# Hash-bucket attention and a channel mix on one core: the first two pairs of heads turned in float16 instead of float32, with a new written-out order

## The chip, the cores and the metric

The kernel runs on one core of one Trainium2 chip. The metric is the time of one execution on the device in microseconds (us), as the median of several runs. The engines are called TensorE (PE in the profile), VectorE (DVE), ScalarE (ACT), GpSimd (POOL) and SyncE (SP, which issues most of the DMAs).

## What is computed

The inputs `q`, `k`, `v` are 4 batches x 8 heads x 768 positions x 64 dimensions, in float32. Each row of `q` and `k` gets six bits, the signs of its products with the columns of `proj`; a row of `q` sees only those rows of `k` whose six bits are the same. The result goes through a channel mix with a squared ReLU and a gate.

```python
q_bits = np.einsum('bhsd,dk->bhsk', q, proj) > 0      # and k_bits in the same way
mask = q_bucket[:, :, :, None] == k_bucket[:, :, None, :]
scores = np.where(mask, q @ k.T / 8, -1e9)
x = softmax(scores) @ v                                # heads side by side: 768 x 512 per batch
xk, xr = mixes of x with x shifted by one position
out = sigmoid(xr @ w_r) * (relu(xk @ w_k) ** 2 @ w_v)
```

## The kernel before

**Pairs.** The work goes by 16 pairs of heads (`n` = 0 to 15, four pairs to a batch). A pair has a `q` side and a `k` side with two heads each (`j` = 0, 1). For each pair an operand tile `a` is made that holds, per head, dimensions down the partitions and 768 positions along the row, in float16. Partitions 0 to 63 hold the rounded value ("hi", for `q` and `k` alike four times the input). Of partitions 64 to 127, six hold the bits as large numbers of either sign, so that one product gives score and mask at once: where all six bits agree, a large constant is added, and `exp` with a bias takes it away again; where one differs, `exp` gives nothing.

**Making `a`, pairs 2 to 15.** `add_prep` (L390): VectorE writes "hi" (L398) and what the rounding left, "lo" (L401), into a tile `nh` with positions down the partitions; a DMA transpose (L405) turns `nh` into `a`. `add_bits` (L414): TensorE multiplies `a` (hi and lo) with the negated `proj`, in tiles of 32 columns side by side (L427), VectorE cuts the signs out of PSUM (L431, tile `bx`), and GpSimd copies six rows per head and side over rows of "lo" in `a` (L443), four copies a pair.

**Making `a`, pairs 0 and 1.** `add_prep_turn` (L446) does not use the DMA transpose: TensorE turns the float32 input (L478), ScalarE copies it out of PSUM (L483), TensorE multiplies it with `pw`, a float32 `proj` for two heads side by side (L489), VectorE cuts the signs (L497) straight into the places of the bits in `nh`, beside "hi" (L467), and TensorE turns `nh` in float16 (L512). VectorE or ScalarE copies that to `a` (L517, L519). So there are no row copies for these two pairs, and no "lo".

**Scores and attention.** `add_scores` (L530): nine steps a pair of 1024 columns of PSUM each (L544), and for each an `exp` on ScalarE (L548) that gives the step's PSUM banks free. `add_pv` (L556): the products with `v` and a column of ones (L571), division (L582 to L589), and the turn back (on TensorE for pairs 0 to 3 and 15, L599). The sums of `v` behind L566 and L374 are made by GpSimd (L350 to L362). `add_mix` (L623): the mixes `xk` and `xr` of a pair, on VectorE.

**Channel mix.** `add_moe` (L648), once a batch has its four pairs: `w_k` (L659), ReLU (L663), square (L666), `w_r` (L679), tanh (L682), `w_v` (L692), last product (L699), output DMA (L702).

**Order.** Every operation is recorded by `add` (L98) with its engine. `ORDER` (L17) is a list, written out, of all operations; each engine runs its own operations in that order and waits for what it depends on. `BANKS` (L72) gives each group of results its place in the eight banks of PSUM, so a product also waits until the place's former tenant has been read. In `ORDER` of the kernel before, the first product of `w_k` of batch 0 comes when 50 of the 144 score steps have been issued, and the score steps go on between the products after that. At the start and in a few places later TensorE multiplies zeros into an unused bank (L246, 14 times one product, and L251, eight times two).

Of the kernel before, what the change touches and what calls it, by code (L numbers as in the profile page):

```python
# [8 lines left out]
FP32 = mybir.dt.float32  # L9
FP16 = mybir.dt.float16  # L10
BF16 = mybir.dt.bfloat16
U16 = mybir.dt.uint16
# [57 lines left out]
]  # L70

BANKS = [  # L72
# [706 lines left out]
```

## Time and profile before

| what | value |
|---|---|
| median of three runs | 242.76 us (242.56 to 243.35) |
| the profiled execution | 242.0 us |
| its span, first to last instruction | 240.2 us |
| TensorE busy | 234.1 us |
| ScalarE busy | 181.9 us |
| VectorE busy | 179.8 us |
| GpSimd busy | 99.7 us |
| granted TensorE clock | 1.0 in every slice |

Around the span of the profiled execution lie 1.8 us, and it took 0.8 us less than the median. Busy time of TensorE is read with care: its matmuls overlap, and their ends are modelled, so what tells of TensorE is the distance from one matmul's start to the next. Rows of the chain of waits give that distance, since they are merged along the chain; rows of the groups give the mean of one instruction from start to end.

### The profile page before, as it was taken

The page shows a single profiled execution, that of the slowest core. Times are in us where ns is not written, and L with a number is a line of the kernel's source. Part 1 is how long each engine was busy: PE and PEld are TensorE (multiplying, and loading weights), DVE is VectorE, ACT ScalarE, POOL GpSimd, SP SyncE. Part 2 cuts the span into 40 slices and gives each one's busy share as a digit, 9 for nine tenths or more (in the row PEclk, how much of TensorE's full clock was granted, in tenths as well). Part 3 has the DMA queues.
Part 4 walks back from the last instruction along what each step waited for, and adds up shares of the span by engine and source line. Part 5 has one row for each costly group of instructions (what it writes and reads, how often), then busy time and mean ns, then how long its engine had stood idle before and what let it go on. Part 6 is the DMA issues. An engine that isn't in the chain of part 4 may idle for free.

```text
span 240.2 us, 6251 instructions
## 1 busy us (share of the span) xinstructions
PE 234.1 (97%) x2515; PEld 147.8 (62%) x2532; DVE 179.8 (75%) x388; ACT 181.9 (76%) x242; POOL 99.7 (41%) x148
## 2 busy tenths in 40 slices
PE   8999999999999999999999999999999999999994
PEld 6985776776766565656456656665566564455442
DVE  3488789999998898989868896887167867348232
ACT  2699999999999999889779999677884640256320
POOL 4064979989934899438087302550000000000000
PEclk9999999999999999999999999999999999999999
DMA  6989999999999999988999989401500401210333
GB/s 225 304 222 274 232 242 260 279 197 362 279 253 284 273 213 294 249 302 206 276 163 241 249 177 234 136 0 26 173 0 3 120 3 44 87 46 1 131 135 131
DMA packets 72605, 44.00 MB, mean 183 GB/s; under 512 B 54912, under 2 KB 67584, under 8 KB 72576
## 3 DMA queue, kind: packets, MB, share of 16 engines
q1 hardware_dynamic: 72208, 43.20, 70.9%
q8 instruction: 20, 0.33, 0.6%
q10 hardware_dynamic: 368, 0.39, 0.5%
q14 instruction: 9, 0.07, 0.1%
HBM read 24.12 MB, written 6.29 MB: 127 GB/s over the span
## 4 chain that ended last, share of the span: by engine, by line
PE 92%; ACT 5%; issue 1%; DVE 0%
PE ps_all L544 25%; PE ps_all L692 17%; PE ps_all L659 16%; PE ps_all L571 14%; PE ps_all L679 8%; ACT pt L548 4%; PE ps_all L427 4%; PE ps_all L489 2%; PE ps_all L512 1%; PE ps_all L478 1%; ACT kr L663 1%; PE ps_all L251 1%; PE ps_all L246 1%; PE ps_all L599 1%; PE ps_all L566 1%
## 5 line engine op out<-in xcount | busy, mean ns | idle before, releaser
L548 ACT ACTIVATE pt<-ps_all 128x1024 bf16<-128x1024 f32 x144 | 138.4, 1041 | 10.9 <-PE ps_all L544 10.3
L544 PE MATMUL ps_all<-a 128*128 128x256 f16 (+1 forms) x384 | 79.2, 325 | 0.5 <-ACT pt L548 0.3
L443 POOL COPY a<-bx 6x384 f32<-6x384 f32 x56 | 38.9, 695 | 34.4 <-DVE bx L431 19.6
L544 PEld LDWEIGHTS <-a 128*128 128x128 f16 x384 | 34.0, 98 | 23.5 <-issue 4.6
L659 PE MATMUL ps_all<-xk,wk 128*128 128x384 bf16 x256 | 48.3, 326 | 0.1
L571 PEld LDWEIGHTS <-pt 128*128 128x128 bf16 x1152 | 42.5, 97 | 8.0 <-issue 0.5
L692 PE MATMUL ps_all<-wv,k 128*128 128x512 bf16 (+2 forms) x199 | 45.6, 362 | 0.5
L571 PE MATMUL ps_all<-va,pt 128*128 128x65 bf16 x1152 | 44.8, 193 | 0.0
L663 ACT ACTIVATE kr<-ps_all 128x384 bf16<-128x384 f32 x64 | 29.4, 491 | 16.0 <-PE ps_all L659 14.4
L659 PEld LDWEIGHTS <-wk 128*128 128x128 bf16 x256 | 24.2, 98 | 17.0 <-issue 0.6
L692 PEld LDWEIGHTS <-k 128*128 128x128 bf16 x208 | 19.3, 98 | 18.9 <-issue 0.3
L699 DVE SCALAR_TENSOR_TENSOR os<-rs,ps_all 128x512 f32<-128x512 f32 (+2 forms) x26 | 16.5, 643 | 19.0 <-PE ps_all L692 13.7
L682 ACT ACTIVATE rs<-ps_all 128x512 f32<-128x512 f32 x24 | 14.3, 602 | 20.5 <-PE ps_all L679 14.1
L666 DVE TENSOR_TENSOR k<-kr 128x384 bf16<-128x384 bf16 x64 | 23.2, 389 | 8.3 <-ACT kr L663 8.3
L401 DVE SCALAR_TENSOR_TENSOR nh<-nat,nh 128x1536 f16<-128x1536 f32 (+1 forms) x16 | 27.0, 1694 | 0.2
L679 PE MATMUL ps_all<-wr,xr 128*128 128x512 bf16 x88 | 23.2, 379 | 0.4
L356 POOL TENSOR_TENSOR vt<-vn 128x384 f32<-128x384 f32 x12 | 17.8, 1485 | 12.5 <-DMA vn<-in_v_dram 11.7
L589 DVE TENSOR_TENSOR ob<-ps_all,rc 128x384 bf16<-128x384 f32 x32 | 17.5, 553 | 1.4 <-DMA xt<-ob 0.8
L431 DVE TENSOR_SCALAR bx<-ps_all 128x768 uint16<-128x768 uint16 x14 | 13.4, 956 | 5.3 <-PE ps_all L427 4.7
L398 DVE TENSOR_SCALAR nh<-nat 128x1536 f16<-128x1536 f32 (+1 forms) x16 | 15.8, 985 | 0.3 <-PE ps_all L512 0.2
L679 PEld LDWEIGHTS <-xr 128*128 128x128 bf16 x96 | 9.0, 98 | 9.0
L380 DVE SCALAR_TENSOR_TENSOR va<-ps_all,vn 128x384 bf16<-128x384 f32 x24 | 12.7, 548 | 0.5 <-PE ps_all L375 0.2
(77 smaller groups left out, 188.9 us busy)
## 6 DMA issues: line engine op xcount, KB each, us to landing
vn<-in_v_dram SPq DMA_DIRECT2D x16, 384.0 KB, 5.1
out_dram<-os SPq DMA_DIRECT2D x23, 256.0 KB, 2.3
nat<-in_k_dram SPq DMA_DIRECT2D x15, 384.0 KB, 4.7
nat<-in_q_dram SPq DMA_DIRECT2D x15, 384.0 KB, 5.2
wst<-in_moe_w_k_dram SPq DMA_DIRECT2D x2, 512.0 KB, 7.0
wst<-in_moe_w_r_dram SPq DMA_DIRECT2D x2, 512.0 KB, 5.8
wst<-in_moe_w_v_dram SPq DMA_DIRECT2D x2, 512.0 KB, 4.4
k<-in_moe_w_k_dram SPq DMA_DIRECT2D x1, 512.0 KB, 4.4
```

Of the source, the lines that this page charges most:

```text
L356: e.tensor_tensor(out=vt[:, :, :, 0:E], in0=src[:, :, 0:3, 0:E], in1=src[:, :, 3:6, 0:E], op=ALU.add)
L401: nc.vector.scalar_tensor_tensor(out=nh[:, :, D:P], in0=nat.rearrange("p j (c d) -> p (j c) d", d=D), scalar=QS, in1=nh[:, :, 0:D], op0=AL ...
L443: nc.gpsimd.tensor_copy(side_a[side][n % NAQ][D : D + NB, j, :].bitcast(FP32), bx_t[sx][32 * i : 32 * i + NB, :].bitcast(FP32))
L544: nc.tensor.matmul(ps[:, lo - s * STEP : hi - s * STEP], side_a["k"][sa][:, j, jc * P : (jc + 1) * P], side_a["q"][sa][:, j, q0 : q0 + hi ...
L548: nc.scalar.activation(out=pt_t[sp][:, s * STEP : (s + 1) * STEP], in_=ps_t[plan.slot[nm]], func=AF.Exp, bias=EBIAS, scale=ESC)
L571: nc.tensor.matmul(oo[:, ic * 65 : ic * 65 + 65], pt_t[sp][:, o : o + P], va_t[sa][:, j, jc, 0 : D + 1], start=(not uc and ic == 0 and jc ...
L589: nc.vector.tensor_tensor(out=ob_t[so][:, :, j * D : (j + 1) * D], in0=oo[:, :, 0:D], in1=rc_t[sr][:, 1, :].unsqueeze(2).to_broadcast([P, ...
L659: nc.tensor.matmul(ps[:, 0:HALF], wk_sb[:, d, fc * P : (fc + 1) * P], xk_t[mx[d]][:, h * HALF : (h + 1) * HALF], start=(d == 0), stop=(d = ...
L663: nc.scalar.activation(out=kr_t[sk], in_=sm(nm)[:, 0:HALF], func=AF.Relu, scale=0.5 ** 0.5)
L666: nc.vector.tensor_tensor(out=k2_t[s2][:, h * HALF : (h + 1) * HALF], in0=kr_t[sk], in1=kr_t[sk], op=ALU.mult)
L679: nc.tensor.matmul(sm(nr), xr_t[mx[d]][:, c * P : (c + 1) * P], wr_sb[:, d, :], start=(d == 0), stop=(d == NDC - 1))
L692: nc.tensor.matmul(sm(nv)[:, x0:x1], k2_t[(b * NFC + fc) % NK2][:, c * P : (c + 1) * P], wv_sb[:, fc, x0:x1], start=(fc == 0), stop=(fc == ...
```

## The change

`add_prep_turn` and all that it used go: the float32 turns (L478), their copies by ScalarE (L483), the float32 products (L489), the sign cuts (L497), the float32 identity, two clearings of `pw`, two clearings of `nh` by VectorE (L265), and the `exp` of a small tile on ScalarE at the start (L253). Six of the 14 single products of zeros go; the eight double ones stay.

Pair 0 is made by a new function, one head at a time. VectorE writes "hi" of `q` and ScalarE "hi" of `k`; VectorE writes "lo" of both; TensorE turns each half in float16; VectorE copies `q` and ScalarE `k` to `a`; then `add_bits` runs for that head's two blocks alone.

```diff
+    def add_prep_first():
+        nat, nh, a = ({x: t[x][0] for x in "qk"} for t in (side_nat, side_nh, side_a))
+        for j in range(2):
+            for side in "qk":
+                e = "DVE" if side == "q" else "ACT"
...
+                def lo(n_=n_, h_=h_):
+                    nc.vector.scalar_tensor_tensor(out=h_[:, :, D:P], in0=n_, scalar=QS, in1=h_[:, :, 0:D], op0=ALU.mult, op1=ALU.subtract)
+
+                def tp(nm=nm, h_=h_):
+                    ps = sm(nm)[:, 0:HALF].bitcast(FP16)
+                    for c in range(NSC):
+                        nc.tensor.transpose(ps[:, c * P : (c + 1) * P], h_[:, c, :], idh)
...
+            add_bits((0,), [("q", j), ("k", j)])
```

Pair 1 goes through `add_prep` and `add_bits` like the later pairs, except that TensorE turns `nh` and VectorE copies it to `a`, where the others use the DMA transpose:

```diff
+            if n in TURNED:
+                for j in range(2):
...
+                    add("PE", 0.48, tp, r=["idh", ("nhh", side, sh, j), ("nhl", side, sh, j)], w=[(nm,)], take=("sm", nm, 0), name=nm)
+                    add("DVE", DVE_C(S, 2), ev, r=[(nm,)], w=[("a", side, sa, j)] + [("ab", side, sa, j, h) for h in range(2)], give=[nm], name="ev" + nm)
+                continue
...
-    NWARM = 14
+    NWARM = 8
...
-    FIRSTS = (0, 1)
+    TURNED = (1,)
```

`ORDER` and `BANKS` are new as a whole. What stands in them where the steps of the prediction lie:

- VectorE at the start: "hi" of `q` (head 1), its "lo", "hi" of `q` (head 0), "lo" of `k` 0, `q` 0 and `k` 1, two copies of turned tiles, "hi" and "lo" of pair 1 (`q`), the first sign cut of pair 0, "hi" of pair 2 (`q`), the second sign cut, a copy, "hi" and "lo" of pair 1 (`k`), a copy, "hi" of pair 2 (`k`), two copies, two "lo" of pair 2, the sign cut of pair 1.
- GpSimd: after the constants the five small operations on `proj`, four row copies of pair 0, the sums of `v` of pair 0, a cast of `v` of pair 1, four row copies of pair 1, and on as before.
- ScalarE: "hi" of `k` twice, two copies, and then nothing but `exp` until the first ReLU. Before, one of the float32 copies stood between the `exp` steps of pair 0.
- SyncE: pair 0 and `proj` first as before; then `q` of pair 1, `v` of pair 0, `q` of pair 2, `k` of pair 1, `k` of pair 2.
- TensorE: the first product of `w_k` comes when 54 of the 144 score steps have been issued, and its bank is that of the step whose `exp` is the 52nd. Ahead of it stand also three groups of 12 products with `v` and one pair of small products (L374, L375) that stood behind it before; no other kind of work has changed sides of it. Before, the order past that point was another one too; the operations past it are the same otherwise.
- The last products are those of 256 columns of `w_v` in both orders. Ahead of them stands a product group of 512 columns in the new order.

More of the change, by code (lines that the diff above doesn't have):

```diff
@@ L157 @@
     NPAIRS = B * NPB
-    NWARM = 14
+    NWARM = 8
     NUC = 4
-    TURN = {(n, side, j): ("ACT" if n == 0 else "ACT", "DVE", "DVE", "ACT" if side == "k" and n == 0 else "DVE") for n in range(2) for side in "qk" for j in range(2)}
-    PARTS = {0: ((0, 1), (1, 2)), 1: ((0, 2),)}
     W_CAST = ["POOL"] * 10
     MERGED = tuple(range(4, 16))
-    FIRSTS = (0, 1)
+    TURNED = (1,)
     JOINT = ()
@@ L241 @@
     wz = k2_all[:, (NK2 - 1) * S + S - 512 : NK2 * S]
-    tb = buf([P, 2], FP32, "tb")
     add("DVE", 0.2, lambda: nc.vector.memset(wz, 0.0), w=["wz"])
-    add("POOL", 0.1, lambda: nc.gpsimd.memset(tb, 0.0), w=["tb"], port=1, name="ctb")
     for i in range(NWARM):
@@ L252 @@
         add("PE", 0.218, filler, r=["wz"], w=[f"warmb{i}"], take=("sm", f"warmb{i}", 0), give=[f"warmb{i}"], name=f"warmb{i}")
-    add("ACT", 1.5, lambda: nc.scalar.activation(out=tb[:, 0:1], in_=tb[:, 1:2], func=AF.Exp), r=["tb"], w=["tb0"], at=0.75, name="table")
     add("POOL", 0.5, lambda: make_identity(nc, idh), w=["idh"], port=1, name="cidh")
@@ L260 @@
     add("POOL", 0.1, lambda: nc.gpsimd.memset(tiny, TINY), w=["tiny"], port=1, name="ctiny")
-    add("POOL", 0.6, lambda: make_identity(nc, idf), w=["idf"], port=1, name="cidf")
-    for e in range(2):
-        add("POOL", 0.1, lambda e=e: nc.gpsimd.memset(pw[e * D : (e + 1) * D, (1 - e) * NB : (2 - e) * NB], 0.0), w=[f"pwz{e}"], port=1, name=f"cpw{e}")
-    for i in range(NNH):
-        add("DVE", 0.8, lambda i=i: nc.vector.memset(nh_t[i][:, :, D + NB : P].bitcast(FP32), 0.0), w=[("nz", i)], name=f"nz{i}")
     for i in range(NVA):
@@ L417, in add_bits @@
         nbits[0] += 1
-        nm = f"bits{n}"
+        nm = f"bits{n}" + ("" if len(blocks) == 4 else str(blocks[0][1]))
         rows = 32 * len(blocks)
@@ new lines, in add_prep_first, with hi @@
+                e = "DVE" if side == "q" else "ACT"
+                nm = f"t0{side}{j}"
+                n_ = nat[side][:, j, :].rearrange("p (c d) -> p c d", d=D)
+                h_ = nh[side][:, j * NSC : (j + 1) * NSC, :]
+                a_ = a[side][:, j, :]
+                def hi(n_=n_, h_=h_, e=e):
+                    if e == "DVE":
+                        nc.vector.tensor_scalar(out=h_[:, :, 0:D], in0=n_, scalar1=QS, scalar2=None, op0=ALU.mult)
+                    else:
+                        nc.scalar.activation(out=h_[:, :, 0:D], in_=n_, func=AF.Copy, scale=QS)
@@ new lines, in lo, with ev @@
+                def lo(n_=n_, h_=h_):
+                    nc.vector.scalar_tensor_tensor(out=h_[:, :, D:P], in0=n_, scalar=QS, in1=h_[:, :, 0:D], op0=ALU.mult, op1=ALU.subtract)
+                def tp(nm=nm, h_=h_):
+                    ps = sm(nm)[:, 0:HALF].bitcast(FP16)
+                    for c in range(NSC):
+                        nc.tensor.transpose(ps[:, c * P : (c + 1) * P], h_[:, c, :], idh)
+                def ev(nm=nm, a_=a_, e=e):
+                    i_ = sm(nm)[:, 0:HALF].bitcast(FP16)
+                    if e == "DVE":
+                        nc.vector.tensor_copy(a_, i_)
+                    else:
+                        nc.scalar.copy(a_, i_)
@@ new lines, in add_prep_first @@
+                rn, kh, kl = [("nat", side, 0, j)], [("nhh", side, 0, j)], [("nhl", side, 0, j)]
+                add(e, DVE_C(384, 2) if e == "DVE" else ACT_C(384), hi, r=rn, w=kh, port=int(e == "DVE"), name=f"hi0{side}{j}")
+                add("DVE", DVE_C(384), lo, r=rn + kh, w=kl, port=1, name=f"lo0{side}{j}")
+                add("PE", 0.48, tp, r=["idh"] + kh + kl, w=[(nm,)], take=("sm", nm, 0), name=nm)
+                add(e, DVE_C(S, 2) if e == "DVE" else ACT_C(S), ev, r=[(nm,)],
+                    w=[("a", side, 0, j)] + [("ab", side, 0, j, h) for h in range(2)], give=[nm], name="ev" + nm)
@@ L722 @@
             add_proj()
-            add_prep_turn(0)
+            add_prep_first()
         if n < NPAIRS:
@@ L728 @@
             quads = [("q", 0), ("q", 1), ("k", 0), ("k", 1)]
[L729 to L731 removed]
+            if n + 1 in JOINT:
                 add_prep(n + 1)
```

77 lines of the change are left out of this document (6 added, 71 removed), and 119 rows, old and new, of tables (BANKS, ORDER).

## Prediction

> **What bounds the kernel now.** I read the page first: its busy times and the shares of the chain that ended last.
>
> ```profile
> span 240.2 us, 6251 instructions
> PE 234.1 (97%) x2515; PEld 147.8 (62%) x2532; DVE 179.8 (75%) x388; ACT 181.9 (76%) x242; POOL 99.7 (41%) x148
> ...
> PE 92%; ACT 5%; issue 1%; DVE 0%
> ```
>
> By that the kernel is TensorE's, and less work for TensorE is time won. But it is an average over stages. So I read the busy time by stretches, cut where the order changes its character: at 57.6 us the first product of `w_k` starts. Columns: stretch, its length, then busy time and instructions of each engine.
>
> ```profile
> 20.90:57.60 36.70, 36.67 (x588) 25.32 (x586) 33.83 (x59) 36.49 (x41) 30.24 (x36) 1.00 1.10 259
> 57.60:90.00 32.40, 31.96 (x395) 21.02 (x394) 30.36 (x61) 31.91 (x44) 23.59 (x26) 1.00 1.12 269
> 90.00:236.70 146.70, 145.78 (x1365) 85.17 (x1379) 103.01 (x242) 99.20 (x141) 36.32 (x53) 1.00 0.53 139
> ```
>
> Up to 57.6 us ScalarE is as full as TensorE (36.49 of 36.70 us), and VectorE has 33.83. Past 90 us TensorE alone is full. In the timeline of ScalarE the first stage is one unbroken row of `exp`; in that of TensorE stand its ends:
>
> ```profile
> 11.60 4.69 ACT L548 ACTIVATE pt<-ps_all 128x1024 bf16<-128x1024 f32 x5
> 16.13 0.85 ACT L483 ACTIVATE pt<-ps_all 128x768 f32<-128x768 f32 x1
> 16.82 2.00 ACT L548 ACTIVATE pt<-ps_all 128x1024 bf16<-128x1024 f32 x2
> 19.06 35.03 ACT L548 ACTIVATE pt<-ps_all 128x1024 bf16<-128x1024 f32 x38 [0.24 <-PE ps_all L544]
> 54.31 6.52 ACT L548 ACTIVATE pt<-ps_all 128x1024 bf16<-128x1024 f32 x7 [0.21 <-PE ps_all L544]
> ```
>
> ```profile
> 10.97 0.59 PE L544 MATMUL ps_all<-a 128*128 128x512 f16 x2
> ...
> 57.64 0.65 PE L659 MATMUL ps_all<-xk,wk 128*128 128x384 bf16 x3
> ```
>
> An `exp` starts every (35.03 - 1.04)/37 = 0.918 us (1.04 is the mean of one). Counting through, the 8th starts at 19.06, the 10th, which is the first of pair 1, at 20.90, and the 52nd ends at 54.31 + 6.52 = 60.83. So this stage has ScalarE's pace, and TensorE's work in it is not what sets its length. The end of the kernel is then: **start of the `w_k` products, plus TensorE's work behind that point, plus a tail.**
>
> **The change on TensorE.** Rows of the chain of waits (start, length, what), which give distances between starts:
>
> ```profile
> 1.79 0.64 PE ps_all L246 x3
> ...
> 3.93 1.00 PE ps_all L246 x6
> 4.93 0.22 PE ps_all L251 x2
> ...
> 15.10 0.70 PE ps_all L478 x6
> 15.80 0.34 PE ps_all L512 x6
> 16.14 0.43 PE ps_all L544 x3
> ...
> 17.34 1.24 PE ps_all L489 x12
> ...
> 21.60 0.76 PE ps_all L427 x16
> ...
> 26.32 0.37 PE ps_all L571 x12
> ```
>
> Groups by line and shape give the counts:
>
> ```profile
> L489 PE MATMUL ps_all<-pw,pt 128*128 128x12 f32 x48 | 5.9, 255 | 0.0
> ...
> L478 PE MATMUL ps_all<-pt,nat 128*128 128x128 f32 x24 | 3.2, 275 | 0.0
> ```
>
> Removed: 48 x 1.24/12 = 5.0 us and 24 x 0.70/6 = 2.8 us, and six zero products (0.11 to 0.21 each, about 0.9). Added: bits for pairs 0 and 1. Pair 1 costs 0.76. Pair 0 has two groups of two blocks; I take 0.76 each as well, because the four blocks of today's group run side by side, so that half the blocks save nothing (if they ran one behind the other, 0.38). Net, TensorE has about 6.4 us less to do. None of it lies behind 57.6 us. All comes out of the stage whose length ScalarE sets, or out of the start, before the first score step.
>
> **The start, which the change lengthens and shortens.** Of VectorE and GpSimd (timeline, then groups, then the minimum, median and maximum of all row copies):
>
> ```profile
> 3.98 0.36 DVE L467 TENSOR_SCALAR nh<-nat 128x384 f16<-128x384 f32 x1 [2.12 <-DMA nat<-in_k_dram]
> 5.44 0.58 POOL L710 TENSOR_SCALAR npj<-pw 64x6 f32<-64x6 f32 x2 [2.16 <-DMA pw<-in_proj_dram]
> ...
> 20.70 0.55 DVE L398 TENSOR_SCALAR nh<-nat 128x768 f16<-128x768 f32 x1
> 21.28 0.96 DVE L401 SCALAR_TENSOR_TENSOR nh<-nat,nh 128x768 f16<-128x768 f32 x1
> 22.49 0.96 DVE L431 TENSOR_SCALAR bx<-ps_all 128x768 uint16<-128x768 uint16 x1 [0.24 <-PE ps_all L427]
> ...
> 23.36 0.95 DVE L401 SCALAR_TENSOR_TENSOR nh<-nat,nh 128x768 f16<-128x768 f32 x1
> 23.58 4.82 POOL L443 COPY a<-bx 6x384 f32<-6x384 f32 x4 [2.77 <-issue]
> 24.39 1.10 DVE L398 TENSOR_SCALAR nh<-nat 128x1536 f16<-128x1536 f32 x1
> 25.52 1.94 DVE L401 SCALAR_TENSOR_TENSOR nh<-nat,nh 128x1536 f16<-128x1536 f32 x1
> ```
>
> ```profile
> L517 DVE COPY a<-ps_all 128x768 f16<-128x768 f16 x6 | 3.3, 546 | 0.7 <-PE ps_all L512 0.4
> ```
>
> ```profile
> L443 POOL COPY a<-bx x56: 497/506/1922, 23.6 to 159.1; 6x384 f32<-6x384 f32 x56
> ```
>
> A row copy takes 0.50 us, but the four from 23.58 on took 4.82: they stand while VectorE is in "hi" or "lo" (24.39, 25.52), and not beside a sign cut. That decides how the new start goes, since it puts row copies among "hi" and "lo".
>
> The loads, in SyncE's timeline, the groups of its issues, and the stretch from 4 to 6 us:
>
> ```profile
> 2.27 1.09 SPq L330 DMA_DIRECT2D nat<-in_k_dram  x2
> ```
>
> ```profile
> nat<-in_k_dram SPq DMA_DIRECT2D x3, 384.0 KB, 4.8
> ```
>
> ```profile
> 4.00:6.00 2.00, 2.00 (x18) 1.78 (x17) 0.96 (x3) 0.27 (x1) 0.48 (x2) 1.00 1.01 322
> ```
>
> The first whole tile, now `q` of pair 1, lands at 2.27 + 4.8 = 7.1, and each further one 393 KB / 322 GB/s = 1.2 us later: `k` of pair 1, the fourth, at 10.7. They are needed at 7.6 and 11.7 (below), so `v` of pair 0 and `q` of pair 2, which now go ahead of it, cost nothing; that margin of 1 us is their cover.
>
> The walk. The inputs of pair 0 land from 3.8 us on, as now (3.98 above). VectorE: a "hi" 0.36, a "lo" of half the size (no row; between 0.96/2 = 0.48 and 0.55, by the 128x768 row), another "hi", three more "lo", two copies at 0.47 from start to start; GpSimd's five operations on `proj` come between. Done at 7.6. Then the order puts "hi" and "lo" of pair 1, 0.55 + 0.96, ahead of the first sign cut, whose product is ready at 8.6: it runs from 9.0 to 9.95. Then "hi" of pair 2 holds the first row copy to 10.8, the second ends at 11.35, and the first score step is at 11.4 (before: 10.97), the first `exp` at 12.0 (before: 11.60). The float32 copy at 16.13, between the steps, is gone, so nine steps would put the 10th `exp` at 12.0 + 9 x 0.918 = 20.3. But it needs pair 1's row copies. VectorE until then, from 10.35 on: two sign cuts (1.8), four copies (1.9), "hi" twice (1.1), "lo" three times (2.9), holds by GpSimd's copies and sums some 0.5: pair 1's sign cut ends at 18.55. Two row copies, each waiting for a "hi" of pair 3, end at 20.15; the step takes 0.43 and its `exp` starts at **20.85**, as before (20.90). With no copy held, both shift to 20.1; with each row copy at the mean of the four above, 1.2 us, to about 22.8.
>
> **The sum.** The 52nd `exp` ends at 20.85 + 42 x 0.918 + 1.04 = 60.45 (before: 60.83). In the new order the first `w_k` product needs that step's bank, so it starts at 60.5: 2.86 later than 57.64. Ahead of it stand four more steps (0.43 each, 1.73), three groups of 12 products with `v` (0.37 each, 1.10) and a pair of small ones (0.1, an estimate from the turns, 0.34/6 each): 2.93 us of TensorE's work that is then not behind it. Behind it TensorE waits for next to nothing already (57.60:90.00 has 0.44 us idle), so nothing more is to be had there: 2.86 - 2.93 = -0.1. The handover to ReLU on ScalarE, which is tighter when it comes after 52 steps, I put at +0.2 (the gap in row 54.31 is 0.21; bounds 0 and 0.6). The tail:
>
> ```profile
> 236.71 0.42 DVE L699 SCALAR_TENSOR_TENSOR os<-rs,ps_all 128x256 f32<-128x256 f32 x1 [0.43 <-PE ps_all L692]
> ```
>
> Its last pass is of the same width; a 512-wide one and its DMA come just ahead, for which I add 0.1 (bounds 0 and 0.5). Sum: +0.2 us on the profiled execution's 242.0, so 242.2; that execution lay 0.76 below the median of 242.76, so the median should come to **243.0**.
>
> **Rivals.**
>
> *TensorE's work is the bound in the first stage too.* For it speaks 36.67 of 36.70 us busy. Then all removed behind the first score step is won: 2 x 1.24 + 0.70 + three turns of 0.34, less 0.76 for pair 1's bits, is 3.4, less 0.4 for the later first step; 242.8 - 3.0 = 239.8. Against it: in that order the bank of the 52nd step stands in front of `w_k`, and ScalarE's row has no gap to close. 0.12.
>
> *The start goes better.* No copy held, 20.1 for the 10th `exp`, nothing for handover and tail: 0.75 + 0.3 less, 241.9. The copies' maximum of 1.92 us speaks against it. 0.10.
>
> *Row copies late: slower.* Mechanism: GpSimd's copies of pair 1 are held by "hi" and "lo" of pairs 2 and 3, while VectorE is itself held by GpSimd's sums of `v`. It decides once pair 1's second copy ends after 20.2 us; each us later is a us on the whole, because all `exp` behind it are in one row. At 22.8 for the 10th `exp` that is +2: 245.0. For it: 4.82 us for four. 0.28.
>
> *TensorE goes cold: slower.* Its first matmuls ran at half pace (L246: 0.64/3 = 0.21 apart at 1.79, 0.17 at 3.93; then L251, of the same shape, 0.11 at 4.93). Today it has no pause after that. In the new order it has work for some 3.8 of the 6.9 us from 4.5 to 11.4 and stands for 1.5 us just before the first step. At half pace for some 3.4 us from there, the nine steps' 0.43 become 0.87, just under ScalarE's 0.918, but turns and bits of pair 1 double, 0.34 + 0.34 + 0.76 more, on the way to the 10th `exp`: 244.4. The Trainium skill ("TensorE: Matmul & The Clock Gate", Part 1: The HAM clock gate) says that the clock halves after an idle window of about 3.4 us; by that rule a pause of 1.5 us leaves it warm and my sum stands as it is. No run here yet shows what a half-filled stretch does. 0.10.
>
> **How the numbers follow.** A measurement can tell about 0.3% (0.7 us) from no change. No change 0.40, late rows 0.28, cold 0.10, TensorE bound 0.12, better start 0.10. So faster 0.22, same 0.40, slower 0.38. The range of the likeliest case alone is 242.0 to 243.5. The whole reaches up to the late rows (245.0) with the handover at its bound (0.4 more), and down to the better start (241.9) with `exp` at the pace of the row at 54.31, (6.52 - 1.04)/6 = 0.913, which is 0.2 less over 42 steps, and 0.3 for the measurement: 241.4 to 245.4. Left out are the TensorE case and a start later than 22.8.
>
> **What would show it.** Right: the first score step near 11.4, the 10th `exp` near 20.9, the 52nd ending near 60.5 with the first `w_k` product on its heels, and several us of TensorE's time idle between. Wrong: an `exp` row with gaps below 30 us that name row copies (late rows), matmuls of 512 columns 0.43 apart after 10 us (cold), or `w_k` starting at 57 or earlier (TensorE bound).

## The result and the profile after

The median after is 244.52 us (242.76 to 245.66, 20 runs) against 242.66 us before (241.78 to 244.75, 20 runs beside them): a ratio of 1.0071, 95% interval 1.0051 to 1.0090. So the change makes the kernel slower by 0.7%. The forecast was 243.0 us and no change; the time lies in its range, 1.5 us above the forecast. Ratios here and below leave out runs in which the chip was in a slower state; medians are of all runs. The profiled execution of after took 244.61 us with a span of 242.8 us, 2.4 us more than the span that the prediction came to (240.2 + 0.2).

In after the score steps are L506, `exp` L510, `w_k` L621, `w_v` L654, the division L551, the row copies L445, the DMA transposes L393, the sign cut L433, the products for the bits L429, GpSimd's last sum of `v` L350, its casts of weights L292. In the kernels of the runs these lines stand two higher up (L504 for L506; `b3_before_wk_late` has the lines of before, two higher up as well); in `a3_no_bits` those from the scores on stand four further down (L510).

From the page, the span, TensorE's busy time, and the shares of the chain that ended last by engine:

```profile
span 242.8 us, 6173 instructions
PE 231.8 (95%) x2486; PEld 141.2 (58%) x2486; DVE 186.4 (77%) x387; ACT 180.9 (75%) x237; POOL 104.5 (43%) x151
...
PE 66%; ACT 12%; DVE 7%; issue 6%; DMA 6%; SPq 1%; POOL 0%; DVEq 0%; POOLq 0%
```

TensorE had 92% of that chain before and has 66% now; a quarter of that chain now hangs on ScalarE, VectorE and DMAs. VectorE is 6.6 us busier and GpSimd 4.8. The chain says that TensorE stands more; the timeline of ScalarE says where the first stage gets slower:

```profile
12.09 8.39 ACT L510 ACTIVATE pt<-ps_all 128x1024 bf16<-128x1024 f32 x9 [4.22 <-PE ps_all L506]
20.96 25.77 ACT L510 ACTIVATE pt<-ps_all 128x1024 bf16<-128x1024 f32 x28 [0.47 <-PE ps_all L506]
46.92 12.12 ACT L510 ACTIVATE pt<-ps_all 128x1024 bf16<-128x1024 f32 x13 [0.19 <-ACT pt L510]
59.37 3.05 ACT L510 ACTIVATE pt<-ps_all 128x1024 bf16<-128x1024 f32 x3 [0.33 <-PE ps_all L506]
```

The counts say which `exp` heads a row: the 1st, the 10th, the 38th, the 51st. From the 10th to the 37th the row has no gap; the gaps of 0.19 and 0.33 us stand ahead of the 38th and the 51st. The first row of TensorE's score steps and the first of `w_k`:

```profile
11.45 0.60 PE L506 MATMUL ps_all<-a 128*128 128x512 f16 x2 [1.69 <-POOL a L445]
...
61.59 1.14 PE L621 MATMUL ps_all<-xk,wk 128*128 128x384 bf16 x6
```

`w_k` starts 3.95 us later than before (57.64), and from there to the end of the span it is 242.8 - 61.6 = 181.2 us, against 240.2 - 57.6 = 182.6 before. These two numbers, the **start of `w_k`** and the **rest**, are used for every run below. Stretches of after, the first up to the 10th `exp` (start and end, length, then busy time of PE, PEld, DVE, ACT, POOL):

```profile
0.00:20.96 20.96, 16.82 (x181) 11.01 (x182) 17.31 (x28) 12.32 (x15) 13.35 (x35) 1.00 0.86 258
20.96:61.59 40.63, 38.91 (x584) 26.02 (x582) 36.64 (x64) 40.02 (x44) 37.55 (x46) 1.00 1.13 285
61.59:90.00 28.41, 28.04 (x342) 18.41 (x341) 27.31 (x58) 27.93 (x40) 16.11 (x21) 1.00 1.03 207
90.00:120.00 30.00, 28.52 (x340) 17.63 (x337) 25.95 (x53) 25.98 (x33) 17.88 (x23) 1.00 1.11 260
```

And of before, the stretches that answer to the first and the last of them:

```profile
0.00:20.90 20.90, 19.71 (x174) 16.27 (x175) 12.21 (x28) 14.28 (x20) 9.50 (x35) 1.00 0.86 248
90.00:120.00 30.00, 29.79 (x331) 17.89 (x333) 27.39 (x56) 26.55 (x35) 16.12 (x21) 1.00 0.99 266
```

The float32 work that is gone stood ahead of the 10th `exp` (the last of it starts at 18.3 us in before). Up to that `exp` TensorE now stands 20.96 - 16.82 = 4.14 us, where it stood 1.19, although work of pair 0 has moved in; and from there to `w_k`, where the change took no such work away, it stands 1.72 us, where it stood 0.03. Behind `w_k`, up to 120 us, it stands 0.37 + 1.48 = 1.85 us, where it stood 0.44 + 0.21 = 0.65. Its waits from 62 to 110 us in after (engine and tile, what it waited for: total, times, longest):

```profile
PE ps_all L654 <- DVE ob L551: 1.1, 1, 1.1
PE ps_all L429 <- DMA a<-nh: 0.4, 1, 0.4
PE ps_all L506 <- DVE ob L551: 0.3, 1, 0.3
```

The 1.1 us (at 99 us) goes back, by the order of the rows, to SyncE's queue. From the timeline of after, rows of SyncE and the one of VectorE that follows from them:

```profile
80.03 0.58 SPq L285 DMA_DIRECT2D os<-in_moe_w_v_dram  x1
80.74 0.39 SPq L285 DMA_DIRECT2D k<-in_moe_w_v_dram  x1
81.24 7.17 SPq L393 DMA_TRANSPOSE a<-nh  x1
88.46 0.58 SPq L318 DMA_DIRECT2D nat<-in_q_dram  x1
...
95.40 0.96 DVE L386 TENSOR_SCALAR nh<-nat 128x1536 f16<-128x1536 f32 x1 [2.51 <-issue]
```

A DMA transpose issued right behind two 512 KB loads of `w_v` holds the queue for 7.17 us; pair 10's inputs stand behind it, the second of them is issued at 89.49 and lands 5.8 us later, VectorE begins pair 10 at 95.40 after standing for 2.51 us, and its division, which gives TensorE a bank, comes late.

### The profile page after: what moved, and what is told of

The parts are those of the page before. It is cut to its first block, busy times and chain, and to the rows that moved or that the text cites. A ratio compares the mean times of both kernels' runs of the same rounds, so it can differ in the third digit from the quotient of the medians.

```text
span 242.8 us, 6173 instructions
## 1 busy us (share of the span) xinstructions
PE 231.8 (95%) x2486; PEld 141.2 (58%) x2486; DVE 186.4 (77%) x387; ACT 180.9 (75%) x237; POOL 104.5 (43%) x151
## 4 chain that ended last, share of the span: by engine, by line
PE 66%; ACT 12%; DVE 7%; issue 6%; DMA 6%; SPq 1%; POOL 0%; DVEq 0%; POOLq 0%
PE ps_all L654 16%; PE ps_all L621 15%; PE ps_all L506 15%; ACT pt L510 12%; PE ps_all L533 9%; PE ps_all L641 8%; PE ps_all L429 3%; DMA a<-nh 3%; DMA nat<-in_q_dram 1%; DMA nat<-in_k_dram 1%; DVE nh L386 1%; DVE xr L597 1%; DVE xk L597 1%; DVE ob L551 1%; DVE k L628 1%
## 5 line engine op out<-in xcount | busy, mean ns | idle before, releaser
L510 ACT ACTIVATE pt<-ps_all 128x1024 bf16<-128x1024 f32 x144 | 137.7, 1053 | 13.2 <-PE ps_all L506 12.6
L506 PE MATMUL ps_all<-a 128*128 128x512 f16 (+1 forms) x384 | 79.7, 325 | 4.0 <-POOL a L445 1.7
L445 POOL COPY a<-bx 6x384 f32<-6x384 f32 x64 | 48.4, 756 | 41.2 <-DVE bx L433 26.4
L506 PEld LDWEIGHTS <-a 128*128 128x128 f16 x384 | 33.6, 97 | 28.7 <-issue 7.4
L654 PE MATMUL ps_all<-wv,k 128*128 128x512 bf16 (+2 forms) x208 | 46.9, 363 | 1.1 <-DVE ob L551 1.1
L621 PE MATMUL ps_all<-xk,wk 128*128 128x384 bf16 x256 | 47.9, 326 | 0.0
L533 PE MATMUL ps_all<-va,pt 128*128 128x65 bf16 x1152 | 45.8, 193 | 0.2 <-ACT pt L510 0.2
L625 ACT ACTIVATE kr<-ps_all 128x384 bf16<-128x384 f32 x64 | 30.4, 494 | 20.8 <-PE ps_all L621 15.6
L621 PEld LDWEIGHTS <-wk 128*128 128x128 bf16 x256 | 23.9, 98 | 15.9 <-issue 0.3
L654 PEld LDWEIGHTS <-k 128*128 128x128 bf16 x208 | 19.3, 98 | 20.3 <-issue 1.9
L389 DVE SCALAR_TENSOR_TENSOR nh<-nat,nh 128x1536 f16<-128x1536 f32 (+1 forms) x18 | 29.5, 1649 | 0.3
L641 PE MATMUL ps_all<-wr,xr 128*128 128x512 bf16 x96 | 24.3, 379 | 0.0
L344 POOL TENSOR_TENSOR vt<-vn 128x384 f32<-128x384 f32 x12 | 13.7, 1143 | 19.4 <-DMA vn<-in_v_dram 18.9
L433 DVE TENSOR_SCALAR bx<-ps_all 128x768 uint16<-128x768 uint16 (+1 forms) x17 | 16.2, 953 | 4.4 <-PE ps_all L429 1.7
L551 DVE TENSOR_TENSOR ob<-ps_all,rc 128x384 bf16<-128x384 f32 x32 | 17.5, 552 | 0.4
L429 PE MATMUL ps_all<-a,p 128*32 128x512 f16 (+1 forms) x256 | 14.0, 328 | 0.9 <-DVE a L475 0.4
```

What stands on the lines that cost most here:

```text
L389: nc.vector.scalar_tensor_tensor(out=nh[:, :, D:P], in0=nat.rearrange("p j (c d) -> p (j c) d", d=D), scalar=QS, in1=nh[:, :, 0:D], op0=AL ...
L429: nc.tensor.matmul(ps[32 * i : 32 * i + 32, lo:hi], w_, side_a[side][m % NAQ][:, j, lo:hi], start=(x == 0), stop=(x == len(mats) - 1))
L445: nc.gpsimd.tensor_copy(side_a[side][n % NAQ][D : D + NB, j, :].bitcast(FP32), bx_t[sx][32 * i : 32 * i + NB, :].bitcast(FP32))
L506: nc.tensor.matmul(ps[:, lo - s * STEP : hi - s * STEP], side_a["k"][sa][:, j, jc * P : (jc + 1) * P], side_a["q"][sa][:, j, q0 : q0 + hi ...
L510: nc.scalar.activation(out=pt_t[sp][:, s * STEP : (s + 1) * STEP], in_=ps_t[plan.slot[nm]], func=AF.Exp, bias=EBIAS, scale=ESC)
L533: nc.tensor.matmul(oo[:, ic * 65 : ic * 65 + 65], pt_t[sp][:, o : o + P], va_t[sa][:, j, jc, 0 : D + 1], start=(not uc and ic == 0 and jc ...
```

## The experiments

My theory after the result: the new method (how pairs 0 and 1 are made) costs about nothing, as predicted, and what was lost is lost by the new order: by the place of `w_k` and by waits on VectorE and on DMAs further on. The rivals: the method itself costs (more work for VectorE and GpSimd that comes due in any order), or single waits of the trace are the price. Each run was timed in five rounds beside the kernel before, and its ratio is to those runs of before (medians of 243.05 us for the runs a, 242.64 for b, 242.86 for c, 242.81 for d). `w_k` and the rest are read from one trace of each run: up to `w_k` after, `b2_loads_first` and `c1_turn_first` have the same order, and their `w_k` start at 61.59, 60.95 and 61.51, so a difference of 0.6 us in one trace says little.

| run | median, us | ratio to before, 95% | start of `w_k` | rest |
|---|---|---|---|---|
| before | 242.66 | | 57.64 | 182.6 |
| after | 244.52 | 1.0071 (1.0051 to 1.0090) | 61.59 | 181.2 |
| `a1_old_order` | 247.72 | 1.0199 (1.0173 to 1.0224) | 63.10 | 182.4 |
| `a2_wk_late` | 251.18 | 1.0336 (1.0310 to 1.0361) | 68.28 | 181.3 |
| `a3_no_bits` | 243.58 | 1.0007 (0.9985 to 1.0029) | 61.89 | 180.3 |
| `a4_start` | 255.80 | 1.0527 (1.0495 to 1.0558) | 72.08 | 182.4 |
| `b1_seam36` | 245.37 | 1.0111 (1.0086 to 1.0136) | 59.77 | 183.2 |
| `b2_loads_first` | 244.32 | 1.0072 (1.0048 to 1.0096) | 60.95 | 181.3 |
| `b3_before_wk_late` | 245.83 | 1.0138 (1.0112 to 1.0163) | 62.30 | 181.6 |
| `b4_xk1_behind` | 245.90 | 1.0117 (1.0084 to 1.0151) | 62.38 | 181.6 |
| `c1_turn_first` | 248.67 | 1.0245 (1.0222 to 1.0268) | 61.51 | 185.3 |
| `c2_seam36b` | 243.56 | 1.0042 (1.0023 to 1.0060) | 58.48 | 182.9 |
| `d1_seam36c` | 242.86 | 1.0010 (0.9993 to 1.0026) | 58.58 | 182.9 |
| `d2_wk_sooner` | 246.04 | 1.0142 (1.0116 to 1.0168) | 57.31 | 187.1 |

### The new method in the old order

```diff
 ORDER (a1): entries 1 to 150 as in after
-ORDER, entry 151 on, and BANKS: as in after
+ORDER, entry 151 on, and BANKS: as in before
```

> After's code with its new start (the first 150 entries of the written order, up to the first exp of pair 0), and from there on the order and the PSUM places of the kernel before: the first w_k products stand again behind the exps of 50 score steps instead of 54, VectorE's work in its old sequence. My theory (the place of the w_k products in the order, and the waits of TensorE that the new sequence makes around and behind them, cost what the changed method saves; the method itself is as fast as before): first exp at 12.1, tenth at about 20.9, the first w_k product at 57.5 to 58.5, TensorE idle some 6 us more than in before ahead of it, total 242.3 to 243.2. Rival A (the new method itself costs: row copies, sign cuts and the port that GpSimd shares with VectorE slow the stage whatever the order): w_k at 59.5 or later, total 244 to 245. Rival B (TensorE bound in the first stage too, and only the new order wastes the work saved): w_k at 54 to 55, total 239 to 240.

Neither theory had it. The total is 247.72 us, but most of the loss is one wait early on. TensorE's and GpSimd's rows around it:

```profile
26.75 4.20 POOL L443 COPY a<-bx 6x384 f32<-6x384 f32 x4 [2.11 <-issue]
...
29.88 1.74 PE L504 MATMUL ps_all<-a 128*128 128x512 f16 x5 [3.42 <-POOL a L443]
```

The old order asks for pair 2 with the 17th `exp`. The new start makes pair 2's bits later: its four row copies begin at 26.75 (25.51 in after) and take 4.20 us beside VectorE's "hi" and "lo", and TensorE stands 3.42 us; on top of that its granted clock is 0.50 from 30.04 to 33.45 us. In after's order two more steps of pair 1 come first, and that wait is not there. So the method does need a new order at its start, and this seam was a poor one. Behind `w_k` the rest is 182.4 us, the old value.

### The seam where both are in pace

At the 36th `exp` all steps of pairs 0 to 3 are done in both orders, and the 37th starts at 45.65 in after (45.74 before). There the two orders can be joined.

```diff
 ORDER: through the 36th exp as in after
-behind it ORDER and BANKS as in after
+behind it ORDER and BANKS as in before
+c2: of pair 4 step 5, not step 0, stands ahead of the seam
+d1: as c2, and PSUM places 1 and 3 exchanged behind the seam
```

> After's code and order up to the 36th exp (all steps of pairs 0 to 3, the stretch in which after kept pace with before: the 37th exp starts at 45.65 in after, 45.74 in before), and from there on the order and PSUM places of before. My theory (the new method is in pace by then and costs nothing more; what after loses is lost by its order behind that point: the waits between 46 and 60 us, w_k behind 52 exps, the waits behind w_k): first w_k product at 57.5 to 58.2, 182.4 us from there to the end as in before and a1, total 242.3 to 243.2. Rival (VectorE and GpSimd carry a backlog out of the new method, 6.6 and 4.8 us more busy time, that comes due in any order): w_k at 59 or later, total 244 or more.

The total was 245.37 us, but again for a fault of the seam: TensorE stood 0.54 and 1.65 us at 45 and 47 us for banks (0.70 and 1.82 as the expectation below counts it, with the last 0.16 us of the product before), because a step that the new order makes early kept its place until its late turn in the old one.

> The run with the seam at the 36th exp again, with the seam mended: there the score step 0 of pair 4 stood ahead of the seam as in after, and held its PSUM bank over three exps until its own turn in the old order, so that TensorE waited 0.70 and 1.82 us at 45 and 46.5; here step 5 stands in its place, which is the next to be used. My theory (the new method is in pace by then, and only the new order behind it costs): no wait of over 0.5 us at the seam, the 37th exp at 45.6 to 45.8, the first w_k product at 57.6 to 58.4, 182.4 us from there to the end, total 242.3 to 243.1. Rival (the new method's backlog on VectorE and GpSimd comes due in any order): exps with gaps of 1 us or more in all between 46 and 58 us, w_k at 59 or later, total 243.8 or more.

The 37th `exp` at 45.70, the seam's waits down to 0.54 and 0.71 (0.70 and 0.87 in the other count), `w_k` at 58.48, 243.56 us. The total lies between the two theories, with one gap left, 0.68 us ahead of the 39th `exp`: two steps in a row had one place.

> The seam at the 36th exp once more, with the PSUM places behind it exchanged so that two score steps in a row never share one: in the run before this, steps 7 and 4 of pair 4 did, TensorE waited 0.70 us at 45.11 and 0.87 us at 46.85, and the 39th exp came 0.68 us late; the first w_k product stood at 58.48. My theory (in pace at the 36th exp, the new method costs nothing more in the old order): no gap of an exp over 0.3 us from the 10th to the 50th, w_k at 57.6 to 57.9, total 242.4 to 243.0. Rival (backlog of VectorE and GpSimd): the gap at the 39th exp goes, others come, w_k at 58.3 or later, total 243.4 or more.

The total is 242.86 us, a ratio of 1.0010 (0.9993 to 1.0026): no difference to before. The theory's number for `w_k` (57.6 to 57.9) was missed by 0.7 us, and 58.58 by itself would fit the rival; most of the 0.7 is that execution's start. ScalarE's rows show it:

```profile
12.68 8.39 ACT L508 ACTIVATE pt<-ps_all 128x1024 bf16<-128x1024 f32 x9 [4.05 <-PE ps_all L504]
21.55 28.52 ACT L508 ACTIVATE pt<-ps_all 128x1024 bf16<-128x1024 f32 x31 [0.48 <-PE ps_all L504]
50.28 4.69 ACT L508 ACTIVATE pt<-ps_all 128x1024 bf16<-128x1024 f32 x5 [0.21 <-PE ps_all L361]
55.19 6.54 ACT L508 ACTIVATE pt<-ps_all 128x1024 bf16<-128x1024 f32 x7 [0.21 <-PE ps_all L504]
```

The first `exp` is at 12.68 (12.09 in after), 0.6 us later, and the row behind it has gaps of 0.21 us only, as before had one. So the **same method with the old order behind the 36th `exp` costs nothing, and with the new order 0.7%.** The rival of a backlog from the new method falls: VectorE and GpSimd do the same work in both. And TensorE's saving is idle time here too: from 20.90 us to `w_k` it stands 1.62 us. From 62 to 110 us TensorE waits in this kernel for this alone:

```profile
PE ps_all L504 <- ACT pt L508: 0.3, 1, 0.3
```

### The place of `w_k`

```diff
 before (b3), and a1 (a2): in ORDER
-w_k's first product, then steps 3, 5, 2, 1 of pair 5 with their exps among the products
+steps 3, 5, 2, 1 of pair 5 with their exps, then w_k's first product
```

> The kernel before with one thing changed: four score steps of pair 5 and their exps stand ahead of the first w_k product, as many as in after. My theory (TensorE had next to no idle time ahead of w_k, so those steps' 1.73 us go on top and ScalarE's four exps, 0.905 us each, set the place): w_k 3.0 to 3.7 us later than 57.64, the rest 1.2 to 1.73 us shorter than 182.57, total 244.2 to 245.2. Rival (the waits are made up further on, since ScalarE then has less left behind that point): total within 0.5 us of 242.8.

The total is 245.83 us against 242.64 beside it, 3.2 us more, and `w_k` starts at 62.30. That execution's stage began 0.56 us late (its seven `exp` from the 46th on start at 54.87, before at 54.31), so the four steps put `w_k` off by 4.1 us. The rest is 1.0 us shorter, not 1.73. So both terms came out on the bad side, the total is 0.6 us above what was expected, and the rival falls. The waits, 20 to 66 us:

```profile
PE ps_all L542 <- ACT pt L546: 1.9, 2, 1.5
PE ps_all L657 <- ACT pt L546: 0.6, 1, 0.6
```

With nothing but score steps to do, TensorE waits 2.5 us for ScalarE, where `w_k` products stood before.

> The kernel of a1 with one thing changed: four score steps of pair 5 and their exps stand ahead of the first w_k product, as in after (w_k behind 54 steps). My theory (that product can start only when those exps have given their banks back, and what is moved ahead of it is TensorE's time that was idle there, so the rest behind it is shorter by the four steps' 1.73 us and later by four exps' 3.7): w_k about 3.6 us later than in a1, total 1.5 to 2.2 us above a1. Rival A (the waits on VectorE's ob and on GpSimd in the new sequence are the cause, the place of w_k costs nothing): total within 0.5 us of a1, with w_k later but TensorE idle less behind it. Rival B (the place costs all of it, banks freed late as well): over 3 us above a1.

`a2_wk_late` is 3.5 us above `a1_old_order`, with the same waits (1.9 and 0.6 us on ScalarE) and the rest 1.1 us shorter; `w_k` is 5.2 us later, of which about 1.1 us had gathered before the 36th `exp`, where the two kernels do the same: the same 3.42 us wait was followed by half clock for 6.83 us here and for 3.41 in `a1_old_order` (the rows stand in the last section). So it agrees, and is the less clean of the two.

### Single waits taken away

```diff
 ORDER of after, VectorE (b4)
-rc4, xk1, mc5, ob4, rc4, xs3, ob4, df3, xk3
+rc4, mc5, ob4, rc4, ob4, xk1, xs3, df3, xk3
```

> After with one instruction moved: on VectorE the mix xk1 (1.84 us at 54.96, beside GpSimd's work) stands behind pair 4's two divisions ob4, not ahead of them. In after TensorE waited 0.68 us at 56.48 for the PSUM bank that the first ob4 gives back, and the 51st and 52nd exps came 0.33 and 0.08 us late. My theory (that wait is VectorE's order, and the w_k products start with the 52nd exp's end): the wait at 56.5 gone, the 52nd exp ending 0.4 to 0.6 us earlier, w_k at 61.0 to 61.2, total 243.8 to 244.2. Rival (VectorE as a whole is late there, so the wait only moves, to xk3 or the cut of pair 6): w_k at 61.5 or later, total 244.4 to 244.9.

245.90 us: the rival. The wait for `ob` is gone, and there is a longer one for the sign cut of pair 6, which `xk1` now holds:

```profile
PE ps_all L504 <- DVE bx L431: 1.3, 2, 1.2
```

```diff
 ORDER of after, SyncE: b2, then c1
-transpose of pair 8, two loads of w_v, transpose of pair 9, two loads of pair 10
+b2: transpose of pair 8, two loads of pair 10, two loads of w_v, transpose of pair 9
+c1: transpose of pair 8, two loads of pair 10, transpose of pair 9, two loads of w_v
```

> After with one thing moved: the two loads of pair 10's q and k stand on SP's queue ahead of two 512 KB loads of w_v and of the DMA transpose of pair 9, instead of behind these. In after that transpose held the queue for 7.17 us (81.24 to 88.41), the loads landed by 95.4, VectorE's split of pair 10 waited 2.51 us for them, and TensorE then 1.28 us for VectorE (98.81) and 0.53 us for pair 10's transpose (104.86). My theory (those two waits are the price of that place in SP's queue): both gone, from the first w_k product to the end 179.4 to 180.2 us instead of 181.23, total 242.8 to 243.6. Rival A (the queue's time is one of contention and whatever comes later pays it, here the transpose of pair 9 or w_v): waits of the same sum at other places, total 244.2 to 244.8. Rival B (the long transpose was a chance of that one execution): total as after's, 244.5, with the waits absent in both.

244.32 us, as after. The wait at 99 us is gone; in its place TensorE waits for the transpose that now stands behind four loads, which held the queue for 7.40 us. Its waits, 62 to 110 us:

```profile
PE ps_all L427 <- DMA a<-nh: 1.9, 2, 1.5
```

> After with SP's queue in another order at one place: pair 10's two loads, then the DMA transpose of pair 9, then the two 512 KB loads of w_v. With all four loads ahead of it the transpose held the queue for 7.40 us, and TensorE waited 1.70 us at 89.40 for what it brings; with w_v's two ahead of it for 7.17 us. Theory (a transpose issued into the big loads takes half as long again as the 4.2 to 5.1 us of the others, and that is what TensorE waits for behind w_k): the transpose holds the queue for 4.4 to 5.5 us, no wait of over 0.6 us at 85 to 105, from the first w_k product to the end 179.6 to 180.4 us, total 242.8 to 243.6. Rival (the loads moved behind are late in their turn, w_v's casts on GpSimd and then the w_v products): waits of over 1 us behind 95, total 244.2 to 245.

248.67 us: the transpose is down to 4.98 us, as expected, and the rival's price is far above what I gave it. GpSimd's and TensorE's rows:

```profile
81.09 4.98 SPq L391 DMA_TRANSPOSE a<-nh  x1
86.11 1.16 SPq L283 DMA_DIRECT2D os<-in_moe_w_v_dram  x1
87.81 0.37 SPq L283 DMA_DIRECT2D k<-in_moe_w_v_dram  x1
...
93.45 2.59 POOL L290 CAST wv<-k 128x1024 bf16<-128x1024 f32 x1 [5.18 <-DMA k<-in_moe_w_v_dram]
...
98.15 1.07 POOL L443 COPY a<-bx 6x384 f32<-6x384 f32 x2
...
99.27 1.35 PE L504 MATMUL ps_all<-a 128*128 128x512 f16 x6 [4.36 <-POOL a L443]
```

The casts of `w_v` stand ahead of row copies on GpSimd. When the loads land late, the cast waits, the row copies behind it wait, and TensorE stands for 4.36 us. So in the three orders tried this stretch has no slack: whichever of the three is put last, TensorE waits for it. Rival A of `b2_loads_first` (whatever comes later pays) holds, and my theory that those waits could be had by moving a load does not.

### The start

```diff
 add_bits of after (a3): for n < 2 no product, no cut, no row copies
```

> After without the bits products, the sign cuts and the row copies of pairs 0 and 1: their bits are left out, so the scores of these two pairs lack that term; all else stays. My theory (the stage goes at ScalarE's pace from the first exp, so a start that is earlier by some us passes to the end whole, unless VectorE holds it later): first exp at 9 to 10 instead of 12.1, 52nd exp 2 to 3 us earlier, total 241.3 to 242.7. Rival (the middle of the stage is held by VectorE and GpSimd, whose waits at 46 to 59 us stay where they are): first exp as early, but the 52nd at most 1 us earlier, total 243.5 to 244.6.

It does not test what it was meant to: the first `exp` starts at 11.15, but the 10th at 21.48, later than in after. ScalarE, then TensorE, then stretches with the granted clock (the number behind the five busy times):

```profile
11.15 1.02 ACT L514 ACTIVATE pt<-ps_all 128x1024 bf16<-128x1024 f32 x1 [2.96 <-PE ps_all L510]
12.81 1.02 ACT L514 ACTIVATE pt<-ps_all 128x1024 bf16<-128x1024 f32 x1 [0.64 <-PE ps_all L510]
14.44 6.56 ACT L514 ACTIVATE pt<-ps_all 128x1024 bf16<-128x1024 f32 x7 [0.61 <-PE ps_all L510]
21.48 24.93 ACT L514 ACTIVATE pt<-ps_all 128x1024 bf16<-128x1024 f32 x27 [0.48 <-PE ps_all L510]
```

```profile
9.74 0.84 PE L405 MATMUL ps_all<-idh,nh 128*128 128x128 f16 x12 [2.38 <-DVE nh L387]
```

```profile
7.37:10.78 3.41, 1.04 (x14) 0.88 (x15) 3.38 (x5) 0.80 (x1) 2.62 (x3) 1.00 1.07 315
10.78:14.20 3.42, 3.20 (x13) 1.57 (x11) 3.39 (x6) 2.05 (x2) 1.80 (x5) 0.50 1.06 369
```

Without bits to make, TensorE stands 2.38 us, then gets half its clock from 10.78 to 14.20 us, and score steps at half pace do not keep ScalarE fed. Its total, 1.0007, is lower than after's, though its `w_k` is 0.3 us later: the rest is 0.9 us shorter. The order there is after's own, yet TensorE's waits from 62 to 110 us come to 1.1 us in all, not 1.8, and all of it is for row copies, none for the division: the second transpose held the queue for 5.56 us there, not 7.17. So these waits differ from one execution to another, or with what went before; which of the two was not shown.

> The kernel of a1 with the first 20 us in another order: VectorE cuts both halves of pair 0's bits before it splits the rest of pair 1, TensorE puts three score steps of pair 0 ahead of pair 1's turns, and pair 1's bits and cut come ahead of pair 2's low parts. My theory (first stage at ScalarE's pace behind the first exp): first exp at 11.3 to 11.6 instead of 12.1, no gap ahead of the tenth, which starts at 19.7 to 20.2 instead of 20.96, and the total 0.6 to 1.1 us under a1. Rival (pairs 2 and 3, split later, come late in their turn or VectorE is what holds the middle): the same early start, and a total within 0.3 us of a1.

255.80 us, by a fault of my order: the last sum of pair 0's `v`, for which that pair's products with `v` wait, stood behind pair 1's row copies on GpSimd (24.80 us, in after 15.80), and pair 1's turns came late; the clock was at half three times as well. The first `exp`, expected at 11.3 to 11.6, started at 12.77: the row copies stood beside VectorE's "lo". Whether a better start can be had is left open.

### A version to beat both

```diff
 ORDER of d1
-GpSimd: sums 2 and 3 of pair 5's v, casts of w_k;  TensorE: steps 7, 8, 0 of pair 5, then w_k
+GpSimd: casts of w_k, sums 2 and 3;  TensorE: step 7, w_k, step 8, w_k, step 0, w_k; mean of pair 5 behind step 3
```

> The kernel with the mended seam, and the first w_k products moved up: GpSimd casts w_k ahead of the two last sums of pair 5, the mean of pair 5 and what VectorE does with it stand behind the third score step after it, and three w_k groups stand behind the 48th, the 49th and the 50th score step of the first stage, in TensorE's idle time there. Theory (TensorE has idle time in the first stage with the new method, some 0.2 us at each exp, and what the old method filled with turns can now be w_k products): first w_k product at 55.6 to 56.6, the 50th exp not later than in the other run of this call, total 0.5 to 1.0 us below it, 241.6 to 242.4. Rival (the idle time is in pieces of 0.1 to 0.2 us behind each wait for a bank, and a group of 0.49 us in it puts each exp back; or pair 5's late mean holds its v products): w_k as early, but the 52nd exp 0.5 us or more later, total within 0.3 us of the other run or above it.

246.04 us: the rival, 3.2 us above `d1_seam36c`. `w_k` starts at 57.31, 1.3 us sooner than in `d1_seam36c`, and the rest is 4.2 us longer. Some of TensorE's waits, 20 to 66 us:

```profile
PE ps_all L619 <- ACT pt L508: 1.2, 1, 1.2
PE ps_all L619 <- DVE mc L373: 0.8, 1, 0.8
PE ps_all L504 <- DVE ob L549: 0.6, 1, 0.6
```

A bank late, pair 5's mean late, a division late. No kernel here beats before.

## Why the prediction was right and wrong, point by point

**The start: right.** Predicted and measured: first score step 11.4 and 11.45, first `exp` 12.0 and 12.09, 10th `exp` 20.85 and 20.96. The "late row copies" rival did not decide, and VectorE and GpSimd held each other about as reckoned: pair 1's sign cut ended at 18.49, where the walk had 18.55.

**TensorE's saving is not won: right.** Its idle time went from 1.19 to 4.14 us up to the 10th `exp` and from 0.03 to 1.72 us from there to `w_k`, and even with the old order behind it (`d1_seam36c`) the time is that of before. The rival "TensorE bound in the first stage too" (239.8) falls. What carried the forecast, that this stage has ScalarE's pace, holds.

**`w_k` on the heels of the 52nd `exp`, at 60.5: the mechanism right, the size 1.09 us short** (61.59). Of this 0.11 is the 10th `exp`. About 0.33 is my pace: I took 42 x 0.918 = 38.56 from inside one row, but before itself needed 54.31 + 6.52 - 1.04 - 20.90 = 38.89, since its rows are joined by gaps. The other 0.65 is what is left over, and goes with new waits between 46 and 60 us, the largest for VectorE's `ob`. TensorE's waits in after from 40 to 61 us:

```profile
PE ps_all L506 <- DVE ob L551: 0.5, 1, 0.5
PE ps_all L362 <- POOL vs L350: 0.2, 1, 0.2
```

`b2_loads_first`, which does the same up to there, did not have the first of them in its execution, and had `w_k` at 60.95; `b4_xk1_behind` took it away and got another. So it is a stretch with next to no slack, not one place, and some 0.6 of the 1.09 is within what one execution differs from another.

**"Work moved ahead, 2.93, is then not behind it": the step that failed.** With it and 0.3 for handover and tail the rest had to be 182.6 - 2.93 + 0.3 = 179.9 us; it was 181.2. Of those 1.3 us, 1.2 are TensorE's new idle time up to 120 us, 1.85 instead of 0.65 by busy time (by the list of its waits to 110 us it is 1.8 instead of 0.3). I had written that TensorE waits for next to nothing behind `w_k` "already", and so nothing more is to be had; I did not ask whether that holds in another order. It does not: after, `b2_loads_first`, `b4_xk1_behind` and `c1_turn_first`, all with the new order there, wait 1.7 to 4.4 us from `w_k` to 110 us, at different places, and `a3_no_bits` 1.1; `a1_old_order`, `b1_seam36`, `c2_seam36b` and `d1_seam36c`, with the old one, 0.3 each. In the old order too, moving steps ahead gave back only 1.0 of 1.73 us (`b3_before_wk_late`).

**Handover and tail, +0.3: not seen.** From `w_k` to 90 us TensorE stands 0.37 us where it stood 0.44, so no wait for ReLU shows, and the tail got no longer: from its last output pass to the end of the span after takes 242.8 - 239.5 = 3.3 us, before 240.2 - 236.7 = 3.5.

```profile
239.54 0.42 DVE L661 SCALAR_TENSOR_TENSOR os<-rs,ps_all 128x256 f32<-128x256 f32 x1 [0.19 <-PE ps_all L654]
```

Without the 0.3, and with 0.2 for the shorter tail, 1.7 us of the rest have to be found; new idle time gives 1.2 to 1.5 of it, and what is left is open. Busy times can't settle it, since the trace of before lacks some of TensorE's products (2515 of them stand beside 2532 weight loads).

**Cold TensorE: right that it stays warm.** In after its clock is 1.00 in all stretches, with 1.69 us of standing just ahead of the first step; it had 4.75 us of work from 4.5 to 11.4 us, not 3.8. The price that the rival gave was seen in other kernels: in `a3_no_bits`, after 2.38 us, the clock was 0.50. The Trainium skill ("TensorE: Matmul & The Clock Gate", Part 1: The HAM clock gate) gives an idle window of about 3.4 us; the trace shows that such a window need not be empty, for the 3.41 us ahead of the drop in `a3_no_bits` held 1.04 us of work, and the margin that the prediction took from that rule was thinner than it looked: the 3.41 us up to 11.36, just ahead of after's first step, held 1.80.

What stays open: how the 0.7% divides between the place of `w_k` and the waits behind it. The sums above come from one trace. `b3_before_wk_late` and `a2_wk_late` put `w_k` behind 54 steps in the old order, but with a wait of 2.5 us of their own, and lost more than after did; no run kept after's own order up to `w_k` with the old order behind it. And it wasn't shown why TensorE waits less in `a3_no_bits` behind `w_k` than in after.

## What to carry to other kernels

A change of method and a new order in one diff are two changes: cost each by itself, and look for a point at which both orders are in pace, since there the two halves can be joined and run apart. Work moved ahead of a point shortens what is behind it only while nobody behind it comes late, so "it never waits there now" is a fact of the old order and no term of the sum for a new one. In this full schedule a wait that was taken away by moving one instruction came back at another one in all three runs that tried it; look first at what stands behind the thing that is moved.

## What the runs showed that I had not expected

**The clock drops after less standing than I thought, and the same wait can cost more or less.** `a1_old_order` and `a2_wk_late` do the same up to there and have the same wait of 3.42 us, which ends at 29.88 and at 29.83. Stretches of 3.41 us, cut where the granted clock (the number behind the five busy times) changes; first `a1_old_order`, then `a2_wk_late`, then after, around its 1.69 us of standing:

```profile
26.63:30.04 3.41, 0.16 (x1) 0.19 (x2) 2.80 (x2) 1.01 (x2) 3.17 (x3) 1.00 1.18 197
30.04:33.45 3.41, 3.41 (x12) 1.51 (x10) 0.00 (x0) 1.96 (x3) 3.25 (x5) 0.50 1.13 272
```

```profile
25.42:28.83 3.41, 0.64 (x7) 0.36 (x4) 3.18 (x3) 2.17 (x3) 2.08 (x2) 1.00 1.23 168
28.83:32.24 3.41, 2.41 (x8) 1.13 (x8) 0.58 (x1) 1.30 (x2) 3.23 (x5) 0.50 1.15 339
32.24:35.66 3.42, 3.42 (x25) 2.19 (x24) 0.53 (x1) 2.57 (x3) 1.95 (x4) 0.50 0.96 199
```

```profile
7.95:11.36 3.41, 1.80 (x25) 1.12 (x20) 3.41 (x5) 0.00 (x0) 1.44 (x3) 1.00 1.02 311
```

In `a1_old_order` the drop comes 0.16 us after TensorE has begun again, in `a2_wk_late` 1.0 us before. Up to TensorE's last product half clock lasts 3.41 us wherever it comes in these traces, and twice that in `a2_wk_late`. The 3.41 us that end with a drop held 0.16 to 1.15 us of TensorE's work (the upper end in `a4_start`, 36.49 to 39.91); counted in steps of 3.41 us from such a drop, 1.65 us (`a4_start`, 19.43 to 22.84) was enough to keep the clock. Half clock ended after steps with 3.20 us of work or more, and not after the 2.41 of `a2_wk_late`. So a wait of some us costs more than itself, half the pace for 3.41 or 6.83 us on top, and how much depends on where it falls.

**A DMA transpose can hold its queue for 5 us or for 7.** In after one held it for 7.17 us behind two loads of 512 KB, in `b4_xk1_behind` at the same place for 6.86, in `b2_loads_first` for 7.40 behind these and two of 384 KB, and in `c1_turn_first` for 4.98 behind the two of 384 KB alone; all that stands behind it in SyncE's queue is issued that much later. But the loads do not settle it: in `a3_no_bits` the transpose at the same place, behind the same two loads, took 5.56 us, and the one before it, with two loads of 384 KB ahead, 6.22.
